# Loading lambda as one row, and moving block 0's state product, in a fused attention and gated feed-forward kernel

## The chip, the cores and the metric

The kernel runs on one core of one Trainium2 chip. The metric is the device time of one execution in microseconds (us), lower is better. "TensorE" or PE is the matrix engine, PEld its weight loads, DVE is VectorE, ACT is ScalarE, POOL is GpSimd, SP is SyncE. GpSimd issues most loads here; SP and ScalarE issue a few. In this program the products are written to tiles in PSUM, and the other tiles lie in SBUF.

## The reference, cut to what matters

Inputs q, k, v are (4 batches, 8 heads, 768 positions, 64), and each head has a decay `lam` between 0.97 and 0.99. Attention is linear with decay, in blocks, with a state carried from block to block; a feed-forward layer with a sigmoid gate follows.

```python
for b in range(nb):                                   # blocks of the sequence
    intra = (qb @ kb.T) * Dmask                       # lam ** (i - j) for j <= i
    inter = (qb * lam_pow) @ kv_state
    out[:, :, sl] = intra @ vb + inter
    kv_state = lam_block * kv_state + (kb * rev_pow).T @ vb   # decayed k, state product
...
x = out.transpose(0, 2, 1, 3).reshape(B * S, H * D)   # 3072 x 512
return (sigmoid(x @ w_gate) * (x @ w_val)) @ w_out
```

## The kernel before

The kernel takes six blocks of 128 positions. It mixes block n+1's attention into block n's feed-forward layer, so that TensorE always has something to do. A "unit" below is one of the 12 slices of 128 columns of the hidden layer: four gate products, a sigmoid on ScalarE, four value products, and a multiplication of the two on VectorE.

Lambda comes first on SP's queue, spread over 128 partitions by the load itself; the second q of block 0 stands behind it.

```python
lam_bc = const.tile([128, H], FP32, tag="lam_bc")
nc.sync.dma_start(out=lam_bc, in_=lam.partition_broadcast(128))
# ...
q01 = [const.tile([128, H, D], FP32, tag=f"q{b}f", name=f"q{b}f") for b in range(2)]
nc.scalar.dma_start(out=q01[0], in_=q[0, :, 0:C, :].rearrange("h s d -> s h d"))
nc.sync.dma_start(out=q01[1], in_=q[1, :, 0:C, :].rearrange("h s d -> s h d"))
# ...
load(0, "k", 0, 2)            # GpSimd issues these, with a cast to bf16
load(0, "k", 2, 4)
# ... q, v, first gate and value weights
nc.scalar.activation(lnl, lam_bc, AF.Ln)
# ... then Exp for the tables of powers (lamq0, pk, kds, dec)
```

VectorE builds one more table of powers, `lamq`, by doubling. Two small copies seed it.

```python
def make_lamq():
    lp = const.tile([128, HP, C], FP32, tag="lp")
    for u in range(2):
        us = slice(u * 64, (u + 1) * 64)
        nc.vector.tensor_copy(lp[us].rearrange("p (e x) c -> p e x c", e=2)[:, :, :, 0],
                              lam_bc[us, :].rearrange("p (x u e) -> p u e x", u=2, e=2)[:, u])
    w = 1
    while w < C:
        nc.vector.tensor_tensor(out=lp[:, :, w:2 * w], in0=lp[:, :, 0:w], ...)   # cut
        w *= 2
    nc.vector.tensor_copy(lamq, lp)
```

The first units of block 0. `psum()` takes a PSUM buffer from a ring of three.

```python
prod(0, 0, v0)                       # unit 0: sigmoid(gate) * value, VectorE
load_gv(3, GW)
make_kd0(1, nc.gpsimd)               # decayed k of batches 2 and 3
load_gv(4, GW)
# ... loads of block 1, then unit 1:
c(0, 0)                              # state product of batches 0 and 1
v1 = psum()
mm_part(v1, WV, 0, 1, 0, TCH)
prod(0, 1, v1)
make_lamq()
# ... gates of units 2 and 3, values of units 2 and 3, gate of unit 4:
c(0, 1)                              # state product of batches 2 and 3
v4 = psum()
mm_part(v4, WV, 0, 4, 0, TCH)
prod(0, 4, v4)
```

## Time and profile before

| | before |
|---|---|
| median, range | 227.8 us, 227.12 to 227.83 us (3 runs) |
| span of the profiled run | 225.6 us |
| PE busy | 219.2 us |
| block 0's k landed | 8.01 us |
| first gate product | 15.56 us |
| first output product | 63.99 us |
| last product starts | 222.56 us |

The head of the page of the kernel before gives the span, each engine's busy time, and the span in 40 slices (a digit is tenths of busy; PEclk is TensorE's granted clock in tenths).

```profile
span 225.6 us, 4294 instructions
PE 219.2 (97%) x1764; PEld 115.3 (51%) x1764; DVE 104.9 (47%) x192; ACT 79.2 (35%) x149; POOL 79.2 (35%) x75
...
PE   7789999999999999999999999999999999999994
...
PEclk9799999999999999999999999999999999999999
...
q0 software_dynamic: 81232, 13.90, 80.2%
```

TensorE is full from the fourth slice on. The last line is the queue of GpSimd's loads: packets, MB, and the time that its packets took as a share of 16 DMA engines' span.

The wait table of the kernel before, for TensorE (who waited for whom, total us, times, longest):

```profile
PE wm L217 <- DVE ip L124: 1.2, 1, 1.2
PE tq L244 <- DVE qb L500: 0.7, 1, 0.7
PE tq L244 <- ACT qb L165: 0.6, 1, 0.6
PE sp L302 <- DVE QS L262: 0.5, 1, 0.5
PE tk L244 <- DMA kb<-in_k_dram: 0.3, 1, 0.3
```

In these views tq and tk are the transposes of q and k, sp the scores, MT the masked scores, op the attention output and XT its bf16 copy, gp a gate or value product, cp the state product, po an output product, and wm an idle product that only keeps TensorE busy.

All of this is before 12.8 us. So the time is the start of the train of products plus the length of the train, and any gap in it.

The chain that ended last, in its first 16 us (start, length, what):

```profile
1.26 6.75 DMA kb<-in_k_dram
...
8.05 0.63 PE tk L244 x8
...
9.19 1.24 PE sp L302 x16
...
10.44 1.88 DVE MT L197 x3
...
14.93 0.59 ACT XT L354
...
15.56 0.81 PE gp L436 x4
```

The chain begins with a load: block 0's k. The parts that the change touches look so in the list of DMA issues (size, us to landing) and in the timeline (start, length, engine, line, operation):

```profile
lam_bc<-in_lam_dram SPq DMA_DIRECT2D x1, 4.0 KB, 3.7
```

```profile
17.40 1.92 POOL L360 TENSOR_TENSOR kd<-kb,kds 128x1024 bf16<-128x1024 bf16 x1
...
18.36 0.69 DVE L449 TENSOR_TENSOR ht<-sg,gp 128x512 bf16<-128x512 bf16 x1 [1.18 <-ACT sg L444]
...
20.84 0.34 DVE L181 COPY lp<-lam_bc 64x4 f32<-64x4 f32 x2
...
24.37 0.44 PE L406 MATMUL cp<-vb,kd 128*64 128x64 bf16 x16
...
24.77 1.02 PE L436 MATMUL gp<-XT,WV 128*128 128x512 bf16 x4
...
74.44 0.62 PE L302 MATMUL sp<-QS,KR 64*128 64x128 bf16 x16
```

### The profile page before, as it was taken

Reading aid. Unit: us, or ns where it says so; the run is one execution under the profiler, and the core shown is the slowest. Engines: PE = TensorE matmul, PEld = TensorE weight load, DVE = VectorE, ACT = ScalarE, POOL = GpSimd, SP = SyncE. Lnnn points to the kernel's source line nnn. Section 1 sums busy time; section 2 is a strip of 40 time slices with the busy share of each in tenths; the row PEclk is TensorE's granted clock in tenths of the full one; section 3 lists DMA queues with packets and bytes.
Section 4 is the critical chain, followed back from the end, with each engine's and each line's share of the span. In section 5 each row is a group of like instructions: output and inputs, shape, how many; then the busy total and the mean of one; then the engine's idle time right before and its main releaser. Section 6 shows DMA issues by size and latency. Waiting matters only on the chain.

```text
span 225.6 us, 4294 instructions
## 1 busy us (share of the span) xinstructions
PE 219.2 (97%) x1764; PEld 115.3 (51%) x1764; DVE 104.9 (47%) x192; ACT 79.2 (35%) x149; POOL 79.2 (35%) x75
## 2 busy tenths in 40 slices
PE   7789999999999999999999999999999999999994
PEld 2455454788864455444446444446444445444443
DVE  6796746586521522445642345742334850343300
ACT  4474234435432225333115333225333224433221
POOL 8999757993592006940005950000000000000000
PEclk9799999999999999999999999999999999999999
DMA  5999999999999991999021999821820012100022
GB/s 103 156 169 197 191 176 156 134 195 174 157 169 163 207 231 72 214 148 128 2 96 46 163 143 156 53 93 53 187 46 0 0 49 93 49 0 0 0 96 94
DMA packets 105860, 25.72 MB, mean 114 GB/s; under 512 B 95984, under 2 KB 102896, under 8 KB 105840
## 3 DMA queue, kind: packets, MB, share of 16 engines
q0 software_dynamic: 81232, 13.90, 80.2%
q1 hardware_dynamic: 23568, 11.28, 22.3%
q10 hardware_dynamic: 1040, 0.26, 0.5%
q8 instruction: 14, 0.23, 0.4%
q14 instruction: 6, 0.05, 0.1%
HBM read 28.32 MB, written 6.29 MB: 153 GB/s over the span
## 4 chain that ended last, share of the span: by engine, by line
PE 94%; DMA 3%; DVE 1%; issue 0%; ACT 0%; POOLq 0%
PE po L485 27%; PE gp L422 21%; PE vp L428 21%; PE gp L457 5%; PE gp L436 5%; PE vp L463 5%; PE sp L302 3%; DMA kb<-in_k_dram 3%; PE op L314 3%; PE op L326 1%; PE cp L406 1%; PE po L474 1%; DVE MT L197 1%; PE tk L244 0%; ACT XT L354 0%
## 5 line engine op out<-in xcount | busy, mean ns | idle before, releaser
L431 DVE TENSOR_TENSOR ht<-sg,vp 128x512 bf16<-128x512 bf16 x54 | 37.2, 688 | 65.4 <-PE vp L428 65.4
L485 PE MATMUL po<-WO,ht 128*128 128x512 bf16 x276 | 61.9, 379 | 0.0
L422 PE MATMUL gp<-XT,WG 128*128 128x512 bf16 x216 | 55.5, 379 | 0.0
L428 PE MATMUL vp<-XT,WV 128*128 128x512 bf16 x216 | 55.4, 379 | 0.0
L425 ACT ACTIVATE sg<-gp 128x512 bf16<-128x512 f32 x54 | 32.2, 597 | 59.5 <-PE gp L422 59.5
L485 PEld LDWEIGHTS <-ht 128*128 128x128 bf16 x276 | 26.3, 98 | 31.0
L428 PEld LDWEIGHTS <-WV 128*128 128x128 bf16 x216 | 21.2, 98 | 25.5
L422 PEld LDWEIGHTS <-WG 128*128 128x128 bf16 x216 | 20.7, 98 | 24.8
L488 ACT COPY ob<-po 128x512 f32<-128x512 f32 x23 | 13.5, 586 | 52.2 <-PE po L485 50.4
L199 DVE TENSOR_TENSOR MT<-sp,mask 128x512 bf16<-128x512 f32 x40 | 25.2, 683 | 9.9 <-PE sp L302 9.9
L387 POOL TENSOR_TENSOR sd<-Sb,dec 128x512 f32<-128x512 bf16 x8 | 8.1, 1037 | 42.4 <-DVE Sb L413 42.4
L457 PE MATMUL gp<-XT,WG 128*128 128x256 bf16 x96 | 14.4, 273 | 0.0
L463 PE MATMUL vp<-XT,WV 128*128 128x256 bf16 x96 | 14.4, 273 | 0.0
L467 DVE TENSOR_TENSOR ht<-sg,vp 128x256 bf16<-128x256 bf16 x24 | 10.0, 420 | 8.6 <-PE vp L463 8.6
L460 ACT ACTIVATE sg<-gp 128x256 bf16<-128x256 f32 x24 | 9.2, 384 | 13.0 <-PE gp L457 11.8
L96 POOL DMA_DIRECT2D vb<-in_v_dram x10 | 12.9, 1292 | 1.7 <-DMA kb<-in_k_dram 1.1
L378 POOL TENSOR_TENSOR kd<-kb,kds 128x1024 bf16<-128x1024 bf16 x6 | 11.3, 1908 | 4.0 <-DMA kb<-in_k_dram 4.0
L413 DVE TENSOR_TENSOR Sb<-cp,sd 128x512 bf16<-128x512 f32 x8 | 5.2, 686 | 15.5 <-PE cp L406 15.5
L341 ACT CAST XT<-op 128x512 bf16<-128x512 f32 x19 | 9.9, 598 | 2.1 <-PE op L314 2.0
L457 PEld LDWEIGHTS <-WG 128*128 128x128 bf16 x96 | 9.2, 98 | 1.8 <-issue 0.2
L463 PEld LDWEIGHTS <-WV 128*128 128x128 bf16 x96 | 9.4, 98 | 1.1
L77 POOL DMA_DIRECT2D qb<-in_q_dram x8 | 9.4, 1182 | 0.0
(84 smaller groups left out, 161.5 us busy)
## 6 DMA issues: line engine op xcount, KB each, us to landing
out_dram<-ob SPq DMA_DIRECT2D x21, 256.0 KB, 2.0
kb<-in_k_dram POOLq DMA_DIRECT2D x11, 256.0 KB, 10.0
qb<-in_q_dram POOLq DMA_DIRECT2D x9, 256.0 KB, 9.1
vb<-in_v_dram POOLq DMA_DIRECT2D x4, 512.0 KB, 14.4
WO<-in_moe_w_out_dram POOLq DMA_DIRECT2D x3, 512.0 KB, 8.7
WG<-in_moe_w_gate_dram POOLq DMA_DIRECT2D x5, 256.0 KB, 8.5
WV<-in_moe_w_val_dram POOLq DMA_DIRECT2D x5, 256.0 KB, 9.1
qb<-in_q_dram POOLq DMA_DIRECT2D x4, 128.0 KB, 8.9
```

The costliest lines, as they stand in the source:

```text
L96: nc.gpsimd.dma_start(out=lst[n][:, b0:b1], in_=src[b0:b1, :, sl, :].rearrange("b h s d -> s (b h) d"))
L199: nc.vector.tensor_tensor(out=out.rearrange("p (e x) c -> p e x c", e=2), in0=x.rearrange("p (e x) c -> p e x c", e=2), in1=mask.rearrange ...
L378: nc.gpsimd.tensor_tensor(out=KD[n][:, e], in0=K[n][:, e], in1=kds[:, e::2].unsqueeze(1).unsqueeze(3).to_broadcast([128, B, HP, D]), op=AL ...
L422: nc.tensor.matmul(gp, lhsT=WG[:, mt, fs], rhs=x[:, mt, :], start=(mt == 0), stop=(mt == NMT - 1))
L425: nc.scalar.activation(sg, gp, AF.Sigmoid)
L428: nc.tensor.matmul(vp, lhsT=WV[:, mt, fs], rhs=x[:, mt, :], start=(mt == 0), stop=(mt == NMT - 1))
L431: nc.vector.tensor_mul(HT[n, ft], sg, vp)
L436: nc.tensor.matmul(ps[:, lo:hi], lhsT=W[:, mt, ft * 128:(ft + 1) * 128], rhs=x[:, mt, lo:hi], start=(mt == 0), stop=(mt == NMT - 1))
L457: nc.tensor.matmul(gp[:, cs], lhsT=WG[:, mt, fs], rhs=x[:, mt, cs], start=(mt == 0), stop=(mt == NMT - 1))
L463: nc.tensor.matmul(vp[:, cs], lhsT=WV[:, mt, fs], rhs=x[:, mt, cs], start=(mt == 0), stop=(mt == NMT - 1))
L485: nc.tensor.matmul(po, lhsT=HT[n, ft][:, tt * 128:(tt + 1) * 128], rhs=WO[:, ft, :], start=(ft == 0), stop=(ft == NFT - 1))
L488: nc.scalar.copy(ob, po)
```

## The change

The intent: the broadcast of lambda is 128 packets of 32 bytes at the head of a queue (2.09 to 4.12 us in the trace of before); load 32 bytes instead, and spread them over the partitions by a product of a column of ones with the row, in TensorE's idle start. And block 0's second state product, which waited for GpSimd's decayed k, moves forward, to fill TensorE while the next gate weights land; for this VectorE makes the decayed k.

```diff
     lam_bc = const.tile([128, H], FP32, tag="lam_bc")
-    nc.sync.dma_start(out=lam_bc, in_=lam.partition_broadcast(128))
+    lam1 = const.tile([1, H], FP32, tag="lam1")
+    nc.sync.dma_start(out=lam1, in_=lam.partition_broadcast(1))
 ...
+    ones = const.tile([1, 128], FP32, tag="ones")
     nc.vector.memset(zero, 0.0)
+    nc.vector.memset(ones, 1.0)
 ...                       (the identity is made after jn instead of before it)
+    idle(4)                                         # and idle(10) below becomes idle(6)
+    lamp = ps_at.tile([128, H], FP32, name="lamp", tag="ps")
+    nc.tensor.matmul(lamp, lhsT=ones, rhs=lam1, start=True, stop=True)
-    nc.scalar.activation(lnl, lam_bc, AF.Ln)
+    nc.scalar.activation(lnl, lamp, AF.Ln)
 ...
+    nc.scalar.copy(lam_bc, lamp)
 ...
-            pool, tag = (ps_at, "ps") if bp == 0 else (ps_ff, "ff")
+            pool, tag = (ps_at, "ps") if bp == 0 or n == 0 else (ps_ff, "ff")
 ...
     piece_a0(3, True)
+    make_kd0(1, nc.vector)
 ...
     load_gv(3, GW)
-    make_kd0(1, nc.gpsimd)
     load_gv(4, GW)
 ...
     prod(0, 1, v1)
+    c(0, 1)
     make_lamq()
 ...
     sigm(0, 4, g4)
-    c(0, 1)
     v4 = psum()
```

More of the change, by code (lines that the diff above doesn't have):

```diff
@@ L133 @@
         nc.vector.tensor_scalar_add(p1[lo:lo + 32], loc[lo:lo + 32, 0:1], float(lo))
-    nc.vector.tensor_scalar(out=ident, in0=ip1, scalar1=p1, scalar2=None, op0=ALU.is_equal)
     for i, base in enumerate((0.0, float(C))):
@@ L137 @@
                                 op0=ALU.mult, op1=ALU.add)
+    nc.vector.tensor_scalar(out=ident, in0=ip1, scalar1=p1, scalar2=None, op0=ALU.is_equal)
     nc.vector.tensor_scalar(out=tri, in0=ip1, scalar1=p1, scalar2=None, op0=ALU.is_ge)
@@ L152, with idle @@
     load_w(WV, wv_r, 1, GW // 2)
+    wm = ps_ff.tile([128, TCH], FP32, name="wm", tag="ff")
+    def idle(n):
+        for i in range(n):
+            nc.tensor.matmul(wm, lhsT=zero[:, :C], rhs=zero, start=True, stop=True,
+                             skip_group_check=True)
+    idle(4)
+    lamp = ps_at.tile([128, H], FP32, name="lamp", tag="ps")
+    nc.tensor.matmul(lamp, lhsT=ones, rhs=lam1, start=True, stop=True)
     lnl = const.tile([128, H], FP32, tag="lnl")
-    nc.scalar.activation(lnl, lam_bc, AF.Ln)
+    nc.scalar.activation(lnl, lamp, AF.Ln)
     lnp = const.tile([128, HP], FP32, tag="lnp")
@@ L158 @@
         us = slice(u * 64, (u + 1) * 64)
-        nc.scalar.activation(lnp[us, :], lam_bc[us, u::2], AF.Ln)
+        nc.scalar.activation(lnp[us, :], lamp[us, u::2], AF.Ln)
+    nc.scalar.copy(lam_bc, lamp)
     lamq0 = const.tile([128, HP, C], BF16, tag="lamq0")
@@ L211, in transpose @@
             nc.tensor.transpose(out[half(u)], x[:, b, head(g, u), :], ident)
-    wm = ps_ff.tile([128, TCH], FP32, name="wm", tag="ff")
-    def idle(n):
-        for i in range(n):
-            nc.tensor.matmul(wm, lhsT=zero[:, :C], rhs=zero, start=True, stop=True,
-                             skip_group_check=True)
     QS, KS, MT, XT, KD = {}, {}, {}, {}, {}
@@ L497 @@
     load_gv(2, GW)
-    idle(10)
+    idle(6)
     nc.vector.tensor_copy(Q[0][:, 0], q01[0])
```

## The prediction

> **What bounds it.** TensorE. The page's busy table has PE at 219.2 us of a 225.6 us span; the table of stretches shows no PE gap from 16 us to 192 us; the wait table lists 3.3 us of PE waiting, all before 12.8 us. So the change gains only by letting that train of products start earlier, or loses by a gap in it. The chain of waits starts with the load of block 0's k (issued 1.26, landed 8.01 us), then eight transposes, the copy of KS, the scores (9.19), three masked evictions on Vector (to 12.32), the scores of batch 2 (12.70), the copy of XT (14.93), the first product of unit 0 (15.56).
>
> **What the change does.**
> 1. Lambda. Before, the broadcast lands 3.7 us after issue. The trace's DMA records show its 128 packets of 32 B from 2.09 to 4.12 us on the SP queue; q of batch 1, behind them, only starts at about 3.6 and lasts to about 6. There it shares the 16 engines with block 0's k: k moves 290 packets in 5.0-5.5 us and 545 in 5.5-6.0, against 615 per half us alone. [...] With one packet for 128 the second q should be through about 0.8 us earlier, and k catches up most of the 395 packets it lost: I estimate that it lands at 7.6 instead of 8.0, gain 0.4 us (0.15 to 0.6), on the critical path. Lambda should land before 3 us; four idle products end at 2.9, so the ones product should cost TensorE nothing. Ln and Exp on Scalar end at about 5.5 instead of 6.3: no gain of its own, as Vector's first QS waits for q's transposes (6.65).
> 2. k decay on Vector: 1.22 us (its twin's duration) fits into the 1.18 us that Vector waited before the product at 18.36: cost about 0.05, off the path. GpSimd loses a 1.92 us operation and issues loads 2 us earlier, but from 24 us on it waits for landings, so the DMA engines set the pace: no gain.
> 3. State product moved from 24.4 to about 20.1 us: same 0.37 us on TensorE, covers the landing of the next gate weights (20.0). Its Vector copy (0.69 us) now delays the products of units 2 and 3 to about 25; unit 4's value needs the PSUM buffer that unit 2's product frees: a stall of 0 to 0.2 us.
> 4. Clock: half speed from 8.6 to 12.0 us. [...]
>
> **Sum.** -0.4 + 0.1 + about 0 = -0.3 us, and an uncertain -0.2 where the clock stays full: **227.3 us**, 8 in 10 between 226.5 and 228.0. Faster by over 2%: 0.01; within 2%: 0.98; slower: 0.01.
>
> **What would show it.** Right: lambda's landing before 3 us; k's landing 0.2 to 0.6 us earlier with everything up to the first gate product shifted alike; no new PE wait over 0.2 us after 16 us. Wrong: k landing at 8.0 (step 1); a PE gap near 24.8 us or Vector's first product of unit 0 over 0.2 us later (steps 2, 3); earlier loads removing a PE wait that I do not see.
>
> **What would make it wrong.** A late lambda row would hold everything behind it on TensorE; [...] the first transposes slip. Another clock phase could hide or double the gain: the three times of before spread over 0.7 us.

227.8 us of before, less 0.3 us (-0.4 + 0.1 + about 0), less the uncertain 0.2 us where the clock stays full, came to 227.3 us. The 0.2 us was the author's estimate; the trace of before shows the half-speed stretch that it speaks of (8.58 to 12.00 us).

## More of the kernel before

Blocks 2 and later have q and k transposed by DMA; block 2's scores stand between output products:

```python
piece_po(0, 3)
sc(2, 0)             # scores, from QS (transposed q, scaled) and KR (transposed k)
m(2, 0)
piece_po(1, 0)
sc(2, 1)
```

## The result, and the profile after

| | before | after |
|---|---|---|
| median, range (6 runs each, same chip) | 227.8 us, 227.12 to 228.1 | 227.44 us, 227.12 to 227.8 |
| ratio, 95% interval | | 0.9992, 0.9973 to 1.0011 |
| k landed | 8.01 us | 7.43 us |
| first gate product | 15.56 us | 15.04 us |
| first output product | 63.99 us | 63.47 us |
| block 2's first scores | 74.44 us | 74.41 us |
| last product starts | 222.56 us | 222.52 us |

Ratios are the mean time of one kernel's fast runs over that of the other's of the same rounds, so not quite the ratio of the medians. The interval holds 1: no change is shown.

The profile of the changed kernel is more telling than its time: it starts 0.5 us earlier, holds that for 48 us, and has lost it at 74 us. The head of its page:

```profile
span 225.7 us, 4301 instructions
PE 218.7 (97%) x1766; PEld 114.7 (51%) x1766; DVE 106.2 (47%) x194; ACT 79.1 (35%) x150; POOL 77.0 (34%) x74
...
PE   7699999999999999999999999999999999999994
...
PEclk9999999999999999999999999999999999999999
...
q0 software_dynamic: 81232, 13.90, 93.0%
```

The clock stayed full, and the packets of GpSimd's queue took a larger share (93.0% for 80.2%) for the same packets and bytes. TensorE's wait table of the changed kernel:

```profile
PE wm L161 <- DVE zero L124: 1.2, 1, 1.2
PE tk L251 <- DMA kb<-in_k_dram: 0.7, 1, 0.7
PE tq L251 <- DMA qb<-in_q_dram: 0.5, 1, 0.5
PE sp L309 <- DMA KR<-kb: 0.4, 1, 0.4
...
```

Four more lines, of 0.3 us or less and before 12 us, are left out. The fourth line is new, and the only one after 12 us: block 2's scores wait for its transposed k. The timeline of the changed kernel, for the instructions that answer to those shown of before:

```profile
3.01 0.59 PE L166 MATMUL lamp<-lam,ones 1*128 1x8 f32 x2
...
7.48 0.62 PE L251 MATMUL tk<-ident,kb 128*128 128x128 bf16 x8 [0.70 <-DMA kb<-in_k_dram]
...
15.04 0.81 PE L443 MATMUL gp<-XT,WG 128*128 128x384 bf16 x4
...
16.58 1.22 DVE L367 TENSOR_TENSOR kd<-kb,kds 128x1024 bf16<-128x1024 bf16 x1
...
17.84 0.69 DVE L456 TENSOR_TENSOR ht<-sg,gp 128x512 bf16<-128x512 bf16 x1
...
19.53 0.44 PE L413 MATMUL cp<-vb,kd 128*64 128x64 bf16 x16
...
20.92 0.34 DVE L195 COPY lp<-lam_bc 64x4 f32<-64x4 f32 x2
...
24.24 1.02 PE L443 MATMUL gp<-XT,WV 128*128 128x512 bf16 x4
...
74.41 0.62 PE L309 MATMUL sp<-QS,KR 64*128 64x128 bf16 x16 [0.42 <-DMA KR<-kb]
```

The decayed k fits just ahead of unit 0's product. The state product runs at 19.5 us, and unit 4's value follows without a wait. On this reading the first theory was: lambda's row brings 0.5 us, and the wait for block 2's k takes it back. It did not survive the experiments.

### The profile page after: what moved, and what is told of

Its sections match the earlier page's. It is cut to its first block, busy times and chain, and to the rows that moved or that the text cites. A ratio compares the mean times of both kernels' runs of the same rounds, so it can differ in the third digit from the quotient of the medians.

```text
span 225.7 us, 4301 instructions
## 1 busy us (share of the span) xinstructions
PE 218.7 (97%) x1766; PEld 114.7 (51%) x1766; DVE 106.2 (47%) x194; ACT 79.1 (35%) x150; POOL 77.0 (34%) x74
## 4 chain that ended last, share of the span: by engine, by line
PE 66%; DMA 20%; POOL 9%; SPq 2%; issue 1%; DVE 0%; POOLq 0%
PE po L492 22%; PE gp L429 18%; PE vp L435 18%; DMA qb<-in_q_dram 6%; DMA WV<-in_moe_w_val_dram 5%; DMA KR<-kb 5%; DMA kb<-in_k_dram 5%; SPq L242 2%; PE sp L309 2%; POOL WG L103 2%; PE op L321 2%; POOL WV L103 2%; POOL vb L97 2%; PE po L481 1%; POOL kb L97 1%; PE op L333 1%
```

## The experiments

Twelve kernels ran; all gave correct results. They came in three groups on three chips, each with its own runs of before. Kernels that share the first instructions of before or of the changed kernel also serve as further looks at the start, and that turned out to be their main use.

### Group 1: does the wait for block 2's k eat the gain?

**Scores later, in both kernels**

```diff
+    piece_po(1, 0)
     sc(2, 0)
     m(2, 0)
-    piece_po(1, 0)
+    piece_po(1, 1)
     sc(2, 1)
     m(2, 1)
-    piece_po(1, 1)
     piece_po(1, 2)
```

> The changed kernel with block 2's scores one output product (2.6 us) later on TensorE. Main theory (the changed kernel starts its train of products 0.5 us earlier, and gives 0.4 us back waiting for block 2's transposed k before its scores at 74.4 us): that wait is gone, the scores run near 76.5 us with no wait of TensorE before them, and the time is 0.4 to 0.5 us under before, ratio about 0.998. Rival (the early gain is one run's luck of the clock, and the wait costs nothing in the timed runs): ratio as for the changed kernel, 0.999 to 1.000, whatever the order.

Measured: 227.16 us median, ratio 0.9978 (0.996 to 0.9997). The wait before block 2's scores is gone, and the ratio is what the main theory said, though its interval overlaps that of the changed kernel. But the profile shows a second loss that this theory does not have: 49.18 us from the first gate product to the first output product instead of 48.43. Timeline lines of this kernel:

```profile
20.57 1.16 POOL L86 DMA_DIRECT2D kb<-in_k_dram  x1
...
20.81 1.09 DVE L195 COPY lp<-lam_bc 64x4 f32<-64x4 f32 x2
...
24.16 1.28 DVE L456 TENSOR_TENSOR ht<-sg,gp 128x512 bf16<-128x512 bf16 x2
...
24.89 1.02 PE L443 MATMUL gp<-XT,WV 128*128 128x512 bf16 x4 [0.60 <-DVE ht L456]
```

The two small copies took 1.09 us instead of 0.34, VectorE's product of unit 2 came late, and unit 4's value waited for the PSUM buffer that this product frees.

> The same move of block 2's scores in the kernel before. Main theory: before has no wait there (its k lands about 1 us ahead), so nothing is gained: ratio 0.999 to 1.001, span 225.4 to 225.8. Rival (the move is a gain by itself, by some other way): ratio about 0.998, as for the changed kernel with it.

Measured: 227.48 us, ratio 0.9996 (0.9975 to 1.0017), as the main theory had it. But its start, which is instruction for instruction that of before, was not before's: k landed at 7.30 us, the clock stayed full, and the first gate product ran at 14.67 us. That is 0.9 us earlier than in the first profile of before, and 0.4 us earlier than the changed kernel.

**Block 2's q and k ahead of the output weights, in both kernels**

```diff
     make_kd(1)
-    for i in range(3):
-        load_wo(i, NFT // 3)
 ...
-    load(2, "qkv", 0, B)
+    load(2, "qk", 0, B)
+    for i in range(3):
+        load_wo(i, NFT // 3)
+    load(2, "v", 0, B)
```

> The changed kernel with the loads of block 2's q and k issued ahead of the output weights. Main theory: block 2's transposes start some 6 us earlier and land well before 70 us, the wait before its scores is gone, ratio about 0.998. It fails if the first output product at 63.5 us now waits for the output weights; I expect them to land at about 59 us, so no wait. Rival (the wait is not the load's doing, but that of the transposes themselves): the transposed k lands at 74 us as before and the wait stays.

Measured: 227.46 us, ratio 0.9993 (0.9976 to 1.001). The wait is gone, but the ratio of 0.998 did not come. The transposed k landed at 71.9 us, 2.4 us earlier than in the changed kernel, not well before 70 us. Again the copies were long (0.70 us for the first), and unit 4's value came 0.56 us late.

> The same order of loads in the kernel before. Main theory: no wait to remove there, ratio 0.999 to 1.001. Rival (the order helps by itself): 0.998.

Measured: 228.09 us, ratio 1.0012 (0.9991 to 1.0032), so nothing gained. Here too the first gate product ran early (14.91 us), and here too the early start was lost: TensorE's wait table has 0.5 us for the second state product, waiting for a product of VectorE, and 0.3 us for value weights.

### Group 2: which part brings the early start?

**Lambda's part alone**

```diff
  (the changed kernel, with these taken back)
-    make_kd0(1, nc.vector)
+    make_kd0(1, nc.gpsimd)           # after load_gv(3, GW), as before
-    c(0, 1)                          # after unit 1's value
+    c(0, 1)                          # after unit 4's gate, in ps_ff, as before
```

> Only lambda's part of the change: row, ones product, Vector's order; decayed k of batches 2 and 3 on GpSimd and the state product after unit 4's gate, as before. Main theory (the early gain is the 127 packets that no longer stand ahead of the second q): block 0's k lands near 7.45 us, the first gate product starts near 15.0 us, as in the changed kernel; the wait for block 2's transposed k comes back as well. Rival (the k decay and the moved state product bring some of the gain): first gate product at 15.4 or later.

Measured: 227.71 us, ratio 1.0008 (0.9983 to 1.0034). k landed at 7.84 us, not at 7.45; the first gate product ran at 15.39 us. The main theory failed: the row did not bring the early start. The rival's figure (15.4 or later) was all but met, but the next runs do not bear out its cause. No wait for block 2's k came back (its scores were due only at 74.4 us; the transposed k landed at 73.5).

**The other two parts alone**

```diff
  (before, with these)
+    make_kd0(1, nc.vector)           # after piece_a0(3, True); the GpSimd call is gone
+    c(0, 1)                          # after unit 1's value, in ps_at; gone after unit 4's gate
```

> Only the other two parts: decayed k all on Vector and the state product after unit 1's value; lambda by broadcast as before. Main theory: k lands at 8.0 us and the first gate product starts at 15.4 to 15.6 as before; TensorE neither gains nor loses over 0.2 us from there to 60 us; ratio 0.999 to 1.001. Rival: a later start of unit 4's value, or a gain, of more than 0.2 us.

Measured: 227.24 us, ratio 0.9991 (0.9968 to 1.0014). The first gate product ran at 14.67 us, not at 15.4 to 15.6: with the broadcast in place. From there to the first output product it lost 0.37 us, more than the 0.2 us expected, where unit 1's value waited for its weights (landed at 18.50 us).

**The packets put back, beside the row**

```diff
     nc.sync.dma_start(out=lam1, in_=lam.partition_broadcast(1))
+    lamx = const.tile([128, H], FP32, tag="lamx")
+    nc.sync.dma_start(out=lamx, in_=lam.partition_broadcast(128))
```

> The changed kernel with the broadcast put back ahead of the second q, into a tile that nothing reads: row and ones product stay. Main theory: the 128 packets of 32 B run from about 2 to 4.3 us again, the second q is through near 6.2 us, k lands at 7.9 to 8.1 us, and the early gain of 0.5 us is gone (first gate product near 15.5). Rival (the gain comes from Ln and Exp being done earlier on Scalar): k's landing may slip, but the first gate product stays near 15.1 us.

Measured, one look: the second q landed at 6.42 us, against 5.01 us in the changed kernel, so the packets do hold up that q. k landed at 7.84 us and the first gate product ran at 15.32 us. That is near the main theory's numbers, but k landed at 7.84 us without the packets too (lambda's part alone), so this one look does not show that they are the cause.

**More idle products in the start of before**

```diff
-    idle(10)
+    idle(12)
 ...
-    idle(1)                          # twice, before tq of batch 1 and before the scores
+    idle(2)
```

> The kernel before with four more idle products in its first 8.6 us (12 for 10, and 2 for 1 twice), where TensorE waited. Theory of the clock [...]: clock 1.00 for the whole run, scores of batch 0 and 1 in 0.4 us each, first gate product 0.1 to 0.3 us earlier than before's 15.56. Rival (phase is luck, or the start is bound by landings alone): half-speed window as before, or full clock with the first gate product within 0.1 us of 15.56.

Measured: 227.82 us, ratio 1.0016 (0.9995 to 1.0037). The clock was full and the first gate product ran at 14.68 us; but three kernels with the start of before, and no more idle products, had the same (14.67, 14.91, 14.67 us). So the full clock came with and without the added products, and the half-speed stretch was the luck of one profile, as the rival had it: of these five it is in the first of before alone. What the theory named as its cause was not shown. This run has another use. It starts 0.9 us earlier than the first profile of before, and reaches the first output product at 64.06 us, where that reached it at 63.99: the kernel before gives an early start back. Some 0.45 us of it goes to waits for the value weights of unit 1 and the gate weights of unit 2. Its timeline shows where the last part goes:

```profile
20.17 1.09 DVE L181 COPY lp<-lam_bc 64x4 f32<-64x4 f32 x2
...
24.25 0.44 PE L406 MATMUL cp<-vb,kd 128*64 128x64 bf16 x16 [0.23 <-DVE ht L449]
...
24.84 1.02 PE L436 MATMUL gp<-XT,WV 128*128 128x512 bf16 x4 [0.15 <-DVE ht L449]
```

### What the ten profiles say together

First, when the copies are long. In every profile in which one of them is long, it ends when GpSimd ends the issue of a load (within 0.02 us), although the traces show no data or semaphore that joins the two:

| kernel | copy from, to (us) | GpSimd's issue from, to (us) |
|---|---|---|
| scores later, changed | 20.81 to 21.71 | 20.57 to 21.73 |
| q, k first, changed | 21.10 to 21.80 | 20.65 to 21.80 |
| packets put back | 21.20 to 21.65 | 20.50 to 21.66 |
| lambda's part alone | 20.67 to 20.94 | 20.18 to 20.94 |
| q, k first, before | 20.59 to 21.46 | 20.30 to 21.47 |
| more idle products | 20.34 to 21.26 | 20.09 to 21.27 |

Copies that began less than 0.23 us after such an issue began, or between two issues, took their 0.15 to 0.17 us. Three more first copies (in before with scores later, the other two parts alone, and the state product alone) began 0.60 to 0.98 us after an issue had begun, and took 0.16 to 0.18 us: the issue then ended, and they too ended with it, within 0.01 us. So 0.16 us of work took up to 0.92 us. Why is in no trace; what the runs show is the common end, and, in group 3, that the stall goes with the copies. In the first profile of before and in that of the changed kernel both copies happened to fall right, which is why neither showed the loss.

Second, what the row does to the loads. The trace's semaphore records give, for each load, the time at which each of 16 DMA engines was done; the first transpose of k starts after the last (8.05 after 8.01 us in before, 7.48 after 7.43 in the changed kernel). The kernel with the packets put back has the row as well.

| kernel | second q landed | k: first engine, last engine | share of GpSimd's queue |
|---|---|---|---|
| before | 6.63 | 6.74, 8.01 | 80.2% |
| before, scores later | 5.98 | 6.47, 7.30 | 79.8% |
| before, q, k first | 6.02 | 6.74, 7.55 | 79.2% |
| before, more idle products | 6.01 | 6.57, 7.32 | 79.8% |
| other two parts alone | 5.99 | 6.68, 7.31 | 79.9% |
| changed | 5.01 | 6.16, 7.43 | 93.0% |
| changed, scores later | 5.38 | 6.38, 7.35 | 91.0% |
| changed, q, k first | 5.16 | 6.15, 7.58 | 96.7% |
| lambda's part alone | 5.00 | 5.94, 7.84 | 90.7% |
| packets put back | 6.42 | 6.48, 7.84 | 92.9% |

With the row in the packets' place the second q comes about 1 us earlier, and the first engine has its part of k about 0.5 us earlier on the mean (6.16 against 6.64). But the last engine is not earlier, and k is there when the last one is. From the first engine to the last it takes 0.97 to 1.90 us in the five profiles with the row, against 0.63 to 0.83 us in four of the five with the broadcast (1.27 in the first).

The landings also show a load that the theories left out: batch 1's v, which GpSimd issues after k and q. It landed at 12.69 to 13.38 us in all seven profiles with the row, against 12.41 to 12.60 us in six of the seven with the broadcast (13.12 in the first; all 14 profiles counted, with those of group 3). In these six the first gate product ran 7.36 to 7.37 us after k landed. In six of the seven with the row it ran 0.11 to 0.28 us later than that after k, but 2.02 us after batch 1's v landed, and TensorE's attention product of batch 1 ran 0.04 us after that landing. So in these the start waits for v, whose last engine is late as well. In the seventh (seed copies on ScalarE, group 3) v came in time and k landed first of all, at 7.07 us; there VectorE held the start, as it copied KS only at 8.09 us, and the first gate product ran at 14.74 us, no earlier than with the broadcast.

So a new theory: lambda's row is no gain and rather a loss; what limits the changed kernel between 15 and 64 us is the pair of copies.

### Group 3: the new theory

**Seed copies on ScalarE**

```diff
-        for u in range(2):            # in make_lamq, between unit 1 and unit 2
-            nc.vector.tensor_copy(lp[us]..., lam_bc[us, :]...)
+    for u in range(2):                # at the start, after dec
+        nc.scalar.copy(lp[us]..., lam_bc[us, :]...)
```

> The changed kernel with the two small copies that seed lamq's ladder moved from Vector to Scalar, early, beside the other small operations on lambda. New theory: in most runs one of these copies stands on Vector for 0.3 to 0.9 us until GpSimd has finished issuing a load (it ends within 0.02 us of that issue in all six profiles in which it is long), and where that is so, Vector's product of unit 2 comes late and unit 4's value waits for its PSUM buffer (0.10, 0.56, 0.76 us in three profiles). Without the copies on Vector the ladder starts straight after the state's copy, and the stall before unit 4's value is under 0.05 us: 48.4 to 48.6 us from the first gate product to the first output product. Time 0.2 to 0.4 us under the changed kernel, ratio near 0.998. Rival (the ladder itself is blocked as well, or the stall has another cause): a stall of 0.2 us or more stays before unit 4's value.

Measured: 227.49 us, ratio 0.9995 (0.9978 to 1.0013). The stall is gone: 48.42 us from the first gate product (14.74 us) to the first output product (63.16 us). The time did not fall by 0.2 us, though: this profile lost it at the other place, in TensorE's wait table:

```profile
PE sp L309 <- DMA KR<-kb: 0.8, 1, 0.8
```

**Seed copies on ScalarE, and scores later**

> The same, with block 2's scores one output product later too. Both known ways of losing the early start are shut: no wait of TensorE over 0.1 us from the first gate product on, 48.4 to 48.6 us to the first output product, 158.55 us from there to the last product. Ratio 0.997 to 0.998, the fastest with lambda's row.

Measured: 227.39 us, ratio 0.9991 (0.9974 to 1.0008). The mechanism is as expected: after 14 us the wait table has no line for TensorE at all, 48.42 us to the first output product and 158.56 us from there to the last product. The time is not: with both leaks shut, what is left is the start, and the first gate product ran only at 15.02 us.

**The same with the broadcast**

The edits of the last kernel, on top of the kernel with the other two parts alone.

> As the last, but lambda by broadcast as before (no row, no ones product). New theory: the row is no gain, since block 0's k is there when the slowest of 16 engines is done, at 7.35 to 7.85 us in five profiles with the row, against 7.3 to 7.55 in four of five with the broadcast: first gate product near 14.7, some 0.3 us before the one with the row, and a time 0.1 to 0.4 us lower, ratio 0.996 to 0.997. Rival (the row is a gain as predicted): first gate product at 15.0 or later, and slower than the version with the row.

Measured: 226.86 us median (226.74 to 227.33, 6 runs), ratio 0.9972 (0.9953 to 0.9991). It is the fastest kernel here, and one of two whose interval against before leaves out 1. First gate product at 14.70 us, 48.42 us to the first output product, no wait of TensorE after that. On the same chip the mean of its six runs is 226.97 us against 227.42 us for the same kernel with the row: 0.45 us, with a standard error of 0.12 us worked out from the spread of the two groups. So lambda's part costs about 0.45 us in this setting. It rests on this pair: the changed kernel with scores later, which has the row, had a ratio of 0.9978, close to this one, on another chip.

The two profiled runs differ by 0.43 us, and their traces show where. With the row, then with the broadcast:

```profile
12.66 0.80 PE L321 MATMUL op<-MT,vb 128*64 128x128 bf16 x16
...
15.02 0.81 PE L443 MATMUL gp<-XT,WG 128*128 128x384 bf16 x4
```

```profile
12.50 0.64 PE L314 MATMUL op<-MT,vb 128*64 128x128 bf16 x16
...
14.70 0.81 PE L436 MATMUL gp<-XT,WG 128*128 128x384 bf16 x4
```

The start is 0.32 us later: 0.16 us because k landed later (7.50 against 7.33 us), and 0.16 us inside the first group of attention products, which waited for batch 1's v (landed at 13.00 against 12.45 us). The other 0.11 us is at the end: from TensorE's last product to the end of the span it took 2.99 against 2.88 us, as the last store landed later after its issue. That holds throughout: 2.98 to 3.01 us in the six timed kernels with the row, 2.85 to 2.88 us in the seven with the broadcast.

**The moved state product alone**

```diff
+    c(0, 1)                          # after unit 1's value, in ps_at
-    c(0, 1)                          # after unit 4's gate
     # the decayed k stays on GpSimd, lambda's broadcast stays
```

> The kernel before with only the state product moved after unit 1's value; decayed k stays on GpSimd, broadcast stays. New theory: the moved product fills the wait for the gate weights of units 2 and 3, so with an early start (first gate product near 14.7) TensorE loses under 0.5 us on the way to the first output product, where the kernel before lost 0.27, 0.95 and 1.12 us in three profiles. If the decayed k from GpSimd (ready near 19.3 us) comes late, the product waits for it: that would be what the move to Vector is for. Time within 0.15% of before.

Measured: 227.48 us, ratio 0.9993 (0.9973 to 1.0013). First gate product at 14.72 us; 49.01 us to the first output product, so 0.59 us lost, more than expected. The loss is not at the state product, but before it:

```profile
PE gp L436 <- DMA WV<-in_moe_w_val_dram: 0.5, 1, 0.5
```

Unit 1's value waited for its weights. They landed at 18.37 to 18.79 us in four of the seven profiles with the broadcast, which lost 0.20 to 0.54 us there, and at 16.78 to 17.71 us in the other three, the best kernel's among them, and in all seven with the row. So the best kernel's profile without a wait is a draw too, and the early start of the broadcast has a tight place of its own. The state product did not wait for GpSimd's decayed k, so no run shows what making it on VectorE is worth.

### Block 2's transposed k

The last DMA engine was done with it at these times (us), in the kernels with the usual order of loads:

| with the broadcast | landed | with the row | landed |
|---|---|---|---|
| before | 72.80 | changed | 74.36 |
| before, scores later | 71.25 | changed, scores later | 73.77 |
| more idle products | 72.09 | lambda's part alone | 73.53 |
| other two parts alone | 72.82 | seed copies | 74.39 |
| state product alone | 71.75 | seed copies, scores later | 73.88 |
| best kernel | 71.59 | packets put back | 74.06 |

The groups do not overlap. The row makes block 2's transposed k later by some 1.9 us on the mean (74.00 against 72.05). That includes the kernel that has both row and broadcast, so it goes with the presence of the row (or with what comes with it, the ones product and the order on VectorE), not with the absence of the 128 packets. How 32 bytes at 2 us can do this is not shown by any run, and stays open.

## Why the prediction was right or wrong

**The total was right, the sum was not.** The forecast was 227.3 us, within 2%; measured 227.44 us, ratio 0.9992, interval 0.9973 to 1.0011. The range held, but the time of before, 227.8 us, lies in it too: that the total came out is no support for its terms. Of these the large one was wrong, and the two stalls that it lacked or made too small were about as large.

**What bounds the kernel: right.** The train of TensorE takes 48.42 us from the first gate product to the first output product and 158.56 us from there to the last product, in every profile without a stall. What is left for a change of this kind to move is the start, the stalls and, as lambda's row did, the 2.9 to 3.0 us after the last product.

**Step 1, "it lands at 7.6 instead of 8.0, gain 0.4 us": this step failed.** Its first half held: lambda landed at 1.96 us (forecast: before 3), the second q landed 1.6 us earlier in the pair of profiles and about 1 us earlier in the others. In the pair the second half looked right as well (k at 7.43 us). But 8.01 us was a draw. Six kernels with the broadcast landed k at 7.30, 7.31, 7.32, 7.33, 7.35 and 7.55 us; six with the row at 7.07, 7.35, 7.43, 7.50, 7.58 and 7.84. The first engine was done with k about 0.5 us earlier (6.16 against 6.64 us on the mean), but not the slowest, and k is complete with the slowest. So the gain of 0.4 us was the distance of one unlucky profile from the usual. The path was wrong too: with the row the start waited in six of seven profiles for batch 1's v (12.91 to 13.38 us), which the forecast did not name. In the pair the first gate product came 0.52 us earlier: 0.58 from k and 0.19 put down to the clock (step 4), less 0.24 waiting for v. And the row even costs: 0.45 us in the one pair of timed kernels that differ in it alone with both stalls shut.

**Step 2, the decayed k: right.** 1.22 us on VectorE, just ahead of unit 0's product (16.58 to 17.80, the product at 17.84). GpSimd's earlier loads brought nothing to see: in the changed kernel it waited 1.17 us for a landing before the load at 19.76 us.

**Step 3, "a stall of 0 to 0.2 us": the mechanism right, the size wrong.** Unit 4's value does wait for the buffer that unit 2's product frees. The stall was 0 in the profile of the changed kernel, and 0.76, 0.56 and 0.31 us in the three others that have the whole change (scores later; q and k first; packets put back). The term that was mis-sized is VectorE's work before unit 2's product: the forecast counted the state's copy (0.69 us) and did not name the seed copies, which took 0.34 us in the first profile and up to 1.09 us in others, until GpSimd's issue of a load ended. With the copies elsewhere the stall was gone in all three kernels tried.

**Step 4, the clock: right as far as it is shown.** The half-speed stretch of the first profile (8.6 to 12.0 us; mean clock of the profile 0.992) came in none of the other 13 (mean clock 0.998 to 1.000), with and without the change, and more idle products changed nothing. In it 16 score products took 1.22 us; in the changed kernel, at the full clock, two groups of 8 took 0.40 us each. It made part of the late start of that one profile, by estimate the 0.19 us that it has over the others: 7.55 us from k to the first gate product, against 7.36 to 7.37 us in the other six with the broadcast.

**What the forecast did not see**: the wait for block 2's transposed k (0.42 us; 0.82 us in the kernel with the seed copies moved), against its own sign of "no new PE wait over 0.2 us after 16 us". Before had 1.6 us of slack there; the early start used 0.5 us of it, and the later landing 1.6.

**What stays open**: why VectorE's copy ends with GpSimd's issue of a load; why the row spreads the 16 engines, from the first loads to the last store (row, ones product and VectorE's new order were never tried apart); why the value weights of unit 1 come late in some profiles with the broadcast; what making the decayed k on VectorE is worth; and how the two earlier parts share the gain of the best kernel, since by time alone none of the single parts is clear of noise.

## What to carry to other kernels

One profile of a kernel's start is one draw: look at the same instructions in several profiles, with kernels that share the start, before you attribute half a microsecond to a change. List every load that the start waits for, and not only the one that came last before. When a bound engine runs without gaps, write the time as start plus train plus stalls, and find each stall's owner; an earlier start alone is given back at the next tight place. And look whether small VectorE copies fall into stretches in which GpSimd issues loads, if something tight depends on them: here a copy of 0.16 us took up to 0.92 us there, and the stall that followed it was gone once the copies were on ScalarE.
